# Decode block with sliding-window attention: value caches loaded and multiplied four heads at a time instead of two, and the output weights in wide products throughout

## Chip, cores, metric

One core of one Trainium2 chip runs one launch of the kernel. The metric is device time in microseconds (us), the median of several runs. All data is fp32.

## What is computed

Two sequences, one new token each, model width 512. A conditioning vector gives six rows of modulation; then attention over the last 4096 entries of the caches (32 query heads, 8 key/value heads of 128), then a SiLU feed-forward of width 1792.

```python
mod = (silu(c) @ w_mod).reshape(2, 6, 1, 512)          # sa, ca, ga, sb, cb, gb
h = layernorm(x) * (1 + ca) + sa
q = (h @ wq) in 32 heads of 128
k, v = the last 4096 entries of each cache, each of the 8 heads used by 4 query heads
o = softmax(q k^T / sqrt(128)) v
x = x + ga * (o @ wo)
h = layernorm(x) * (1 + cb) + sb
out = x + gb * (silu(h @ w1) @ w2)
```

The caches' windows are 2 x 8 x 4096 x 128 values each, 33.6 MB for keys and as much for values; `wq` and `wo` are 8.4 MB each, `w_mod` 6.3 MB, `w1` and `w2` 3.7 MB each. All of it is read once.

## The kernel before, in words

**The ring.** Nearly everything that is read goes through one tile `slots` of 8 slots of 16 KB per partition (L68). `stream(n)` (L70) hands out the next n slots, aligned to n where n is even. Every load is issued by SP, in program order, and waits there until the instructions that read the slots' former content have ended; a later load cannot pass an earlier one. `w_mod` takes slots 0 to 2, `wq` slots 4 to 7, and then the caches follow.

**The steps.** Attention is cut into 8 steps. A step is two key/value heads of one sequence: `load_pair` (L77) brings 4096 x 2 x 128 values as 32 KB per partition in two slots, partition p holding a run of 64 cache entries of one head. The loop (L477) is a hand-written order on each engine (`inorder` keeps it), with the values one step behind the keys:

- `keys(s, j)` (L356): VectorE turns a quarter of the keys in 32x32 blocks by two stream transposes into a tile kT (pool `ktp`, 4 buffers, L55).
- `scores(s, j)` (L366): four TensorE products of 32 output columns by 512, one for each 32-row stripe of the PSUM tile `s`.
- `maxima(s)` (L382) and `exponentials(s)` (L400): VectorE takes row maxima `mx`; TensorE turns them (`mT`); VectorE joins and spreads them (`mg`, `mrow`); TensorE spreads them over the partitions (`bp`); ScalarE copies that (`bias`) and takes exp into `pr`, with row sums.
- `turn(s)` (L415): VectorE transposes `pr` (`xp`) and spreads it (`zp`); TensorE places it (`pT`, 4 products by 256); ScalarE writes the two masked copies `ptb` (two buffers, one for odd and one for even steps).
- `weighted(s)` (L442): 16 products of 32 columns by 512 of `ptb` and the values, on four 32-column stripes in turn, summed in `o`; ScalarE copies the sum to `ob` at once.
- `collect(s)` (L460): four products of 64 columns by 128 pick each head's rows from `ob` and add them up in `o_all`.

In a round of the loop TensorE does the first quarter of scores of step s, then turn(s-1), collect(s-2), the other three quarters, the maxima and exponentials of s, and then the value products of step s-1 (L477 to L499). So value products run while VectorE and ScalarE are busy with the next step's softmax.

**place(n)** (L312) spreads the queries of key/value heads 4n to 4n+3 over `qbd`; place(1) comes in the round of s = 2.

**The rest.** After the loop, `o_all` is divided by the row sums into `on` (L536), turned to `oTn` (L539 to L543), and TensorE does 6 products whose result nobody reads (`busy(6)`, tile `junk`, L576). `wo` lies in slots 0 to 3: the first 28 of its 32 runs are multiplied 512 wide and added up in four stripes (`acc_o`, L577), the last four in 128-wide pieces straight into `ao` (L586); `gather` (L546) copies `acc_o` out, one half by ScalarE and one by VectorE, and adds the stripes into `ao`. Then follow the second layernorm, `w1` (slots 4 to 6, tile `hid`), SiLU, `w2` (slots 7, 0, 1, 2; tiles `acc_yw`, `acc_y`, `acc_l`), another gather, and the output's DMA (L704).

Of the kernel before, what the change touches and what calls it, by code (L numbers as in the profile page):

```python
# [13 lines left out]
P = 128  # L14
# [9 lines left out]
def adaln_block(  # L24
# [30 lines left out]
    ktp = ctx.enter_context(tc.tile_pool(name="ktp", bufs=4))  # L55
# [21 lines left out]
    def load_pair(cache, s):  # L77


        i, b = divmod(s, B)  # L80
        t = stream(2)
        nc.sync.dma_start(
            t,
            cache[b, 2 * i : 2 * i + 2, SK - W :, :].rearrange("e (u n) d -> u e (n d)", u=P // 2),
        )
        return t
# [16 lines left out]
    for b in range(B):  # L103
# [46 lines left out]
    id16, mix = const([P, 16], "id16"), const([P, 16, 2], "mix")  # L150
# [3 lines left out]
    nc.gpsimd.tensor_mul(  # L154
        mix,
        id16[:, :, None].to_broadcast([P, 16, 2]),
        half[:, None, :].to_broadcast([P, 16, 2]),
    )
    odd = const([P, 2], "odd")
    nc.vector.tensor_reduce(  # L160
        odd, ident.rearrange("p (a r) -> p r a", r=2), axis=AX.X, op=ALU.add
# [13 lines left out]
    selh = const([P, 4, 4 * HQ - 8], "selh")  # L175
    nc.gpsimd.memset(selh, 0.0)
    nc.gpsimd.tensor_copy(
        selh[:, :, 2 * HQ - 8 : 2 * HQ].rearrange("p m (e g) -> p m e g", e=2),
        id4.rearrange("p (e m g) -> p m e g", e=2, g=G),
# [26 lines left out]
    ptb = [const([P, 16, 2, 16], f"ptb{i}") for i in range(2)]  # L206
# [132 lines left out]
    o_all = bank("O", "o_all")[:, :DH]  # L339
# [9 lines left out]
    def fetch(s):  # L349

        if s < STEPS:
            kt[s] = load_pair(k_cache, s)
        if s > 0:
            vt[s - 1] = load_pair(v_cache, s - 1)
# [11 lines left out]
    def scores(s, j):  # L366
# [3 lines left out]
        i, b = divmod(s, B)  # L370
        for c in range(2):
            for e in range(2):
                r, h = 64 * e + 32 * c, 2 * i + e
                inorder(nc.tensor.matmul(  # L374
                    s_ps[s][r : r + 32, :],
                    qbd[h // 4][:, h % 4, b, j, :],
                    kT[s, j][:, 32 * c : 32 * c + 32, e:32:2],
                    start=(j == 0),
                    stop=(j == 3),
                ))  # L380
# [34 lines left out]
    def turn(s):  # L415
# [9 lines left out]
        tp = bank("C", f"pT{s}")[:, : 2 * P]  # L425
        for i in range(4):
            inorder(nc.tensor.matmul(  # L427
                tp[32 * i : 32 * i + 32, :],
                mix.rearrange("p v e -> p (v e)"),
                zp.rearrange("p y t x -> p (y t) x")[:, :, 4 * i : 4 * i + 4],  # L430
                start=True,
                stop=True,
            ))
        for e in range(2):
            inorder(nc.scalar.activation(  # L435
                ptb[s % 2][:, :, e, :],
                tp.rearrange("p (w z) -> p w z", z=16),
                AF.Copy,
                scale=odd[:, e : e + 1],
            ))  # L440

    def weighted(s):  # L442


        o_ps[s] = bank("D", f"o{s}")
        for w in range(16):
            r = 32 * (w % 4)
            inorder(nc.tensor.matmul(  # L448
                o_ps[s][r : r + 32, :],
                ptb[s % 2][:, w].rearrange("p e z -> p (e z)"),  # L450
                vt[s].rearrange("p (c w m f d) -> p c f w m d", c=2, w=4, m=4, f=2)[
                    :, w // 8, w // 4 % 2, w % 4
                ],
                start=(w < 4),
                stop=(w >= 12),
            ))
        o_sb[s] = once.tile([P, 4 * DH], F32, tag="wide", name=f"ob{s}")
        inorder(nc.scalar.copy(o_sb[s], o_ps[s]))  # L458

    def collect(s):  # L460

        i, b = divmod(s, B)
        lo = 2 * HQ - 8 - (HQ * b + 2 * G * i)
        for m in range(4):
            r = 64 * (m % 2)
            inorder(nc.tensor.matmul(  # L466
                o_all[r : r + 64, :],
                selh[:, m, lo : lo + 2 * HQ],
                o_sb[s][:, m * DH : (m + 1) * DH],
                start=(s == 0 and m < 2),  # L470
                stop=(s == STEPS - 1 and m >= 2),
                skip_group_check=True,
            ))

    fetch(0)
    keys(0, 0)
    for s in range(STEPS + 1):  # L477
        if s < STEPS:
            fetch(s + 1)
            scores(s, 0)  # L480
        if s > 0 and s != STEPS - 1:
            turn(s - 1)
        if s > 1:
            collect(s - 2)
        if s == 2:
            place(1)
        if s < STEPS:
            for j in range(1, 4):
                keys(s, j)
                scores(s, j)  # L490
            maxima(s)
            exponentials(s)
        if s < STEPS - 2:
            keys(s + 1, 0)
        if s > 0:
            weighted(s - 1)
        if s == STEPS - 2:
            turn(s)
            keys(s + 1, 0)  # L499
    collect(STEPS - 1)  # L500
# [12 lines left out]

    rx = once.tile([P, B, HKV // 2, 2, G], F32, tag="rx", name="rx")
    for b in range(B):
        nc.vector.tensor_mul(
            rx[:, b],
            rowsum[:, b:STEPS:B, None, None].to_broadcast([P, HKV // 2, 2, G]),
# [3 lines left out]
    for r in (0, 64):  # L522
        nc.tensor.matmul(
            lp[r : r + 64, 0:1],
            rx.rearrange("p b i e g -> p (b i e g)"),
            ones,
            start=True,
            stop=True,
        )
    rl = once.tile([P, 1], F32, tag="rl", name="rl")  # L530
# [201 lines left out]
```

## Time and profile before

| | |
|---|---|
| median of 3 runs | 235.44 us (235.41 to 235.5) |
| profiled execution, first to last instruction (its span; the page lists no other time for it) | 233.7 us |
| TensorE products (PE) | 161.1 us busy, 69% |
| VectorE (DVE) | 115.6 us busy, 49% |
| ScalarE (ACT) | 28.5 us busy, 12% |
| moved by DMA | 97.68 MB, 418 GB/s over the span |
| granted TensorE clock, mean | 0.934 |

PE's busy time counts products that run side by side on different columns once. A product of fp32 values shows as two instructions, so "x32" beside a row of value products means 16 products of the code. PEld are the loads of the stationary operand. A row of the timeline gives start, duration, engine, line, operation, output and inputs, the count merged into the row, and in brackets how long the engine had been idle before and what released it. "The span's start" is time zero of all of them.

### The profile page before, as it was taken

What the parts mean: (1) busy time and instruction counts of PE and PEld (TensorE: products, weight loads), DVE (VectorE), ACT (ScalarE), POOL (GpSimd) and SP (SyncE); (2) the same over time, 40 slices, a digit from 0 to 9 for tenths busy, and PEclk for the clock granted to TensorE, in tenths of its full rate; (3) what the DMA queues carried; (4) which work ended last, traced back from release to release, by engine and by line L of the source; (5) the groups of instructions that cost most, each with busy time, mean ns of one, the idle gap of its engine ahead of it and who ended that gap; (6) DMA issues with size and microseconds to landing.
All of it is one profiled execution on the core that took longest, in us unless ns stands there. A gap on an engine that the chain in (4) does not pass through costs nothing.

```text
span 233.7 us, 2571 instructions
## 1 busy us (share of the span) xinstructions
PE 161.1 (69%) x1070; PEld 43.3 (19%) x1070; DVE 115.6 (49%) x179; ACT 28.5 (12%) x64; POOL 10.5 (4%) x35
## 2 busy tenths in 40 slices
PE   0004916859577839797598749759759779789684
PEld 0001401201111111211120201202112122324222
DVE  0007240278894758695197089259559540101232
ACT  2000210000311120120210201111020120102020
POOL 2004710000000000000000000000000000000000
PEclk9999985979999977999979999988997997999999
DMA  7998998999999999999999999999999999989991
GB/s 269 446 542 359 404 494 359 446 444 421 415 421 449 446 437 415 426 426 446 449 437 409 418 437 449 449 421 412 426 444 449 443 421 437 463 367 437 424 404 57
DMA packets 3794, 97.68 MB, mean 418 GB/s; under 512 B 432, under 2 KB 456, under 8 KB 968
## 3 DMA queue, kind: packets, MB, share of 16 engines
q1 hardware_dynamic: 3768, 97.53, 97.1%
q8 instruction: 8, 0.13, 0.2%
q14 instruction: 2, 0.02, 0.0%
q10 hardware_dynamic: 16, 0.00, 0.0%
HBM read 97.53 MB, written 0.00 MB: 417 GB/s over the span
## 4 chain that ended last, share of the span: by engine, by line
DMA 60%; issue 18%; DVE 14%; PE 6%; POOL 0%; SPq 0%; POOLq 0%; ACT 0%
DMA slots<-in_A_k_cache_dram 22%; DMA slots<-in_A_wq_dram 15%; DMA slots<-in_A_v_cache_dram 12%; DMA slots<-in_B_w_dram 12%; DVE kT L361 11%; PE o L448 2%; PE q L302 2%; DVE zp L420 1%; PE acc_yw L661 1%; DVE xp L418 1%; PE qr L323 0%; PE acc_y L671 0%; DVE qT L315 0%; POOL qg L319 0%; SPq L109 0%
## 5 line engine op out<-in xcount | busy, mean ns | idle before, releaser
L361 DVE STREAM_TRANSPOSE kT<-slots 128x1024 f32<-128x1024 f32 x64 | 73.7, 1212 | 23.7 <-DMA slots<-in_A_k_cache_dram 23.6
L374 PE MATMUL s<-kT,qbd 128*32 128x512 f32 x256 | 68.6, 693 | 19.1 <-DVE kT L361 18.0
L448 PE MATMUL o<-slots,ptb 128*32 128x512 f32 x256 | 30.8, 624 | 2.1 <-DMA slots<-in_A_v_cache_dram 2.1
L374 PEld LDWEIGHTS s<-kT,qbd 128*32 128x32 f32 x256 | 9.6, 113 | 68.4 <-DVE kT L361 63.4
L269 PE MATMUL m_a<-slots,scT 128*32 128x256 f32 x32 | 4.4, 506 | 20.5 <-DVE scT L261 20.5
L302 PE MATMUL q<-slots,hq_T 128*32 128x512 f32 x64 | 8.3, 680 | 7.0 <-DMA slots<-in_A_wq_dram 7.0
L448 PEld LDWEIGHTS o<-slots,ptb 128*32 128x32 f32 x256 | 8.1, 114 | 17.9 <-issue 17.8
L404 ACT COPY bias<-bp 128x1 f32<-128x1 f32 x8 | 1.3, 159 | 77.0 <-PE bp L402 77.0
L384 DVE TENSOR_REDUCE mx<-s 128x1 f32<-128x512 f32 x8 | 5.5, 691 | 9.6 <-PE s L374 9.6
L565 PE MATMUL junk<-quad,id 128*32 128x512 f32 x22 | 10.2, 595 | 0.0
L420 DVE TENSOR_TENSOR zp<-xp,quarter 128x1024 f32<-128x1024 f32 x8 | 9.8, 1225 | 0.2
L435 ACT ACTIVATE ptb<-pT,odd 128x256 f32<-128x256 f32 x16 | 6.7, 472 | 25.6 <-PE pT L427 25.6
L255 DVE STREAM_TRANSPOSE cT<-xc 128x128 f32<-128x128 f32 x1 | 0.4, 401 | 16.7 <-DMA xc<-in_c_dram 16.7
L427 PE MATMUL pT<-zp,mix 128*32 128x256 f32 x64 | 5.7, 428 | 3.6 <-DVE zp L420 3.5
L458 ACT COPY ob<-o 128x512 f32<-128x512 f32 x8 | 4.7, 585 | 26.1 <-PE o L448 26.1
L272 PE MATMUL m_sp<-slots,scT 128*32 128x512 f32 x32 | 7.4, 738 | 0.0
L386 PE MATMUL mT<-ident,mx 128*1 128x128 f32 x16 | 3.0, 270 | 6.3 <-DVE mx L384 6.3
L315 DVE STREAM_TRANSPOSE qT<-q 128x512 f32<-128x512 f32 x2 | 1.4, 717 | 11.7 <-PE q L302 10.2
L418 DVE STREAM_TRANSPOSE xp<-pr 128x512 f32<-128x512 f32 x8 | 5.5, 686 | 3.4 <-ACT pr L406 3.4
L579 PE MATMUL acc_o<-slots,oTn 128*32 128x512 f32 x56 | 6.2, 593 | 0.7 <-DMA slots<-in_A_wo_dram 0.7
L466 PE MATMUL o_all<-ob,selh 128*64 128x128 f32 x64 | 6.0, 316 | 0.8 <-ACT ob L458 0.8
L550 DVE COPY acc_o_sb<-acc_o 128x256 f32<-128x256 f32 x1 | 0.4, 425 | 12.4 <-ACT acc_o_sb L549 12.4
(140 smaller groups left out, 93.8 us busy)
## 6 DMA issues: line engine op xcount, KB each, us to landing
slots<-in_A_k_cache_dram SPq DMA_DIRECT2D x8, 4096.0 KB, 27.4
slots<-in_A_v_cache_dram SPq DMA_DIRECT2D x8, 4096.0 KB, 27.6
slots<-in_w_mod_dram SPq DMA_DIRECT2D x1, 6144.0 KB, 17.1
slots<-in_A_wo_dram SPq DMA_DIRECT2D x1, 6144.0 KB
slots<-in_B_w_dram SPq DMA_DIRECT2D x1, 2688.0 KB
slots<-in_A_wo_dram SPq DMA_DIRECT2D x1, 2048.0 KB, 29.5
slots<-in_B_w_dram SPq DMA_DIRECT2D x1, 2048.0 KB
slots<-in_B_w_dram SPq DMA_DIRECT2D x1, 896.0 KB
```

Of the source, the lines that this page charges most:

```text
L272: nc.tensor.matmul(m_sp[r, :], scT[:, k, :], cd[:, g], start=(k == 0), stop=(k == 3))
L302: nc.tensor.matmul(q_ps[n][32 * g : 32 * g + 32, :], hq_T[:, k, :], wv[:, n, g], start=(k == 0), stop=(k == 3),)
L361: inorder(nc.vector.transpose(kT[s, j][:, 32 * c : 32 * c + 32, :], kt[s].rearrange("p (n j r) -> p j n r", j=4, r=32)[:, j, 32 * c : 32 * ...
L374: inorder(nc.tensor.matmul(s_ps[s][r : r + 32, :], qbd[h // 4][:, h % 4, b, j, :], kT[s, j][:, 32 * c : 32 * c + 32, e:32:2], start=(j == ...
L418: inorder(nc.vector.transpose(xp, pr[s]))
L420: inorder(nc.vector.tensor_mul(zp, xp[:, None, :, 0:16].to_broadcast([P, 4, 16, 16]), quarter[:, :, None, None].to_broadcast([P, 4, 16, 16 ...
L427: inorder(nc.tensor.matmul(tp[32 * i : 32 * i + 32, :], mix.rearrange("p v e -> p (v e)"), zp.rearrange("p y t x -> p (y t) x")[:, :, 4 * ...
L435: inorder(nc.scalar.activation(ptb[s % 2][:, :, e, :], tp.rearrange("p (w z) -> p w z", z=16), AF.Copy, scale=odd[:, e : e + 1],))
L448: inorder(nc.tensor.matmul(o_ps[s][r : r + 32, :], ptb[s % 2][:, w].rearrange("p e z -> p (e z)"), vt[s].rearrange("p (c w m f d) -> p c f ...
L466: inorder(nc.tensor.matmul(o_all[r : r + 64, :], selh[:, m, lo : lo + 2 * HQ], o_sb[s][:, m * DH : (m + 1) * DH], start=(s == 0 and m < 2) ...
L565: inorder(nc.tensor.matmul(junk[0:32, :], id4, quad.rearrange("p m y -> p (m y)"), start=True, stop=True,))
L579: inorder(nc.tensor.matmul(acc[32 * g : 32 * g + 32, :], oTn[:, q, :], wot[q], start=(q < 4), stop=(q >= 24),))
```

## The change

Keys still come two heads at a time, but a step is now two heads of the same sequence as its neighbour (steps 0 to 3 are the first sequence, 4 to 7 the second). Two steps make a group of four heads.

- **Loads.** Values come for four heads in one load of 64 KB per partition in four slots. The ring then holds keys in slots 0 to 3 and values in slots 4 to 7 all through the loop. `fetch_values(i+1)` stands after `weighted(i)`, in the same four slots.
- **Order.** `turn(s)` follows the exponentials of its own step. `weighted(i)` follows the turn of the group's second step, then `collect(i)`, and the next step's keys and scores come after it. `ktp` has 3 buffers instead of 4.
- **turn.** `pT` is 8 products by 256 instead of 4, and the two `ptb` writes of a step are 512 wide instead of 256; `ptb` is one buffer that holds a whole group.
- **weighted.** 32 products of 64 columns by 512, on two 64-column stripes in turn. ScalarE copies the sum to `ob` in four masked pieces of 128.
- **collect.** One product of 64 columns by 512. The four 128-wide pieces are added by one VectorE reduction (`of_all`) after the loop.
- **wo.** All 32 runs are multiplied 512 wide; both halves of each `gather` are copied by ScalarE, with one more unread product after the first one's copies.
- Constants are made to fit (`mix`, `quad4`, `selh`, `own`). place(1) comes in the round of s = 1.

```diff
-    ktp = ctx.enter_context(tc.tile_pool(name="ktp", bufs=4))
+    ktp = ctx.enter_context(tc.tile_pool(name="ktp", bufs=3))
...
+    def load_heads(cache, b, h, heads):
+        t = stream(heads)
         nc.sync.dma_start(
             t,
+            cache[b, h : h + heads, SK - W :, :].rearrange("e (u n) d -> u e (n d)", u=P // heads),
         )
...
+        tp = bank("C", f"pT{s}")
+        for f in range(2):
+            for i in range(4):
+                inorder(nc.tensor.matmul(
+                    tp[32 * i : 32 * i + 32, 2 * P * f : 2 * P * (f + 1)],
...
+    def weighted(i):
...
+        for w in range(32):
+            r = 64 * (w % 2)
             inorder(nc.tensor.matmul(
+                o_ps[i][r : r + 64, :],
+                ptb[:, w].rearrange("p e z -> p (e z)"),
+                runs[:, w // 8, w // 4 % 2, w % 4],
+                start=(w < 2),
+                stop=(w >= 30),
+            ))
...
         for m in range(4):
+            c = slice(m * DH, (m + 1) * DH)
+            inorder(nc.scalar.activation(
+                o_sb[i][:, c], o_ps[i][:, c], AF.Copy, scale=own[:, m : m + 1]
+            ))
...
+        inorder(nc.tensor.matmul(
+            o_all, selh[:, lo : lo + 2 * HQ], o_sb[i], start=(i == 0), stop=(2 * i + 2 == STEPS)
+        ))
...
+    for s in range(STEPS):
+        scores(s, 0)
+        for j in range(1, 4):
+            keys(s, j)
+            scores(s, j)
+        fetch_keys(s + 2)
+        maxima(s)
+        exponentials(s)
+        if s % 2 == 0:
+            keys(s + 1, 0)
+        turn(s)
+        if s == 1:
             place(1)
+        if s % 2:
+            weighted(s // 2)
+            fetch_values(s // 2 + 1)
+            collect(s // 2)
+            if s + 1 < STEPS:
+                keys(s + 1, 0)
...
+    nc.vector.tensor_reduce(
+        of_all, o_all.rearrange("r (m d) -> r d m", m=4), axis=AX.X, op=ALU.add
+    )
...
-    for q in range(28):
+    for q in range(32):
...
-    for q in range(28, 32):
...
-    gather(ao, acc, "acc_o_sb", False, True)
+    gather(ao, acc, "acc_o_sb", True, True, fill=1)
```

How the change moves instructions on TensorE, at the first value products: before (s1 and s2 are the scores of steps 1 and 2, o0 the value products of step 0; the digits behind the last underscore only tell tiles apart):

```order
L374 MATMUL s1_337<-kT1_3_367,qbd0_151 32x512 x4
L386 MATMUL mT1_376<-ident_90,mx1_374 1x128
L402 MATMUL bp1_381<-negscale_141,mrow1_146 128x1
L448 MATMUL o0_390<-slots_80,ptb0_149 32x512 x16
L374 MATMUL s2_411<-kT2_0_387,qbd0_151 32x512 x4
L427 MATMUL pT1_420<-zp1_418,mix_111 32x256 x4
L466 MATMUL o_all_286<-ob0_407,selh_120 64x128 x4
L323 MATMUL qr1_437<-qg1_154,rep4_98 128x128
L374 MATMUL s2_411<-kT2_1_443,qbd0_151 32x512 x4
```

And now, at the first value products (o0 is the first group, steps 0 and 1):

```order
L440 MATMUL pT1_397<-zp1_395,mix_111 32x256 x8
L330 MATMUL qr1_414<-qg1_156,rep4_98 128x128
L462 MATMUL o0_420<-slots_80,ptb_152 64x512 x32
L480 MATMUL o_all_288<-ob0_453,selh_121 64x512
L386 MATMUL s2_463<-kT2_0_460,qbd1_154 32x512 x4
L386 MATMUL s2_463<-kT2_1_468,qbd1_154 32x512 x4
L386 MATMUL s2_463<-kT2_2_475,qbd1_154 32x512 x4
L386 MATMUL s2_463<-kT2_3_482,qbd1_154 32x512 x4
L398 MATMUL mT2_492<-ident_90,mx2_490 1x128
```

The value products stood between a step's softmax inputs (bp1) and its pT, and belonged to the step before. Now they stand behind the pT of their own group's second step, and the next step's first scores stand behind them and behind the collecting product.

On SP, the last loads of the caches and the first of the weights, before:

```order
L82 DMA slots<-in_A_v_cache_dram 128x1x8192
L82 DMA slots<-in_A_k_cache_dram 128x1x8192
L82 DMA slots<-in_A_v_cache_dram 128x1x8192 x2
L93 DMA slots<-in_A_wo_dram 128x12288
L93 DMA slots<-in_A_wo_dram 128x4096
L93 DMA slots<-in_B_w_dram 128x5376
```

And now:

```order
L81 DMA slots<-in_A_v_cache_dram 128x1x16384
L81 DMA slots<-in_A_k_cache_dram 128x1x8192 x2
L81 DMA slots<-in_A_v_cache_dram 128x1x16384
L92 DMA slots<-in_A_wo_dram 128x12288
L92 DMA slots<-in_A_wo_dram 128x4096
L92 DMA slots<-in_B_w_dram 128x5376
```

Before, key and value loads of one size took turns all through the loop. Now two key loads and one value load of twice the size come four times, and each value load stands behind the value products of the group before.

196 lines of the change are left out of this document (75 added, 121 removed).

## The prediction

> **What bounds the kernel now.** First the page's second part, for the shape over time, its third for the queue that loads (packets, MB, share), and its fourth, the chain that ended last.
>
> ```profile
> DMA  7998998999999999999999999999999999989991
> q1 hardware_dynamic: 3768, 97.53, 97.1%
> DMA 60%; issue 18%; DVE 14%; PE 6%; POOL 0%; SPq 0%; POOLq 0%; ACT 0%
> ```
>
> The DMA engines are busy in every slice but the last, and 60% of the chain is waiting for transfers. The windows between landings give the rate (columns: stretch, its length, PE, PEld, DVE, ACT, POOL busy, granted clock, DMA share, GB/s):
>
> ```profile
> 77.10:115.70 38.60, 29.45 (x186) 6.99 (x178) 25.87 (x31) 5.82 (x15) 0.49 (x2) 0.91 1.01 434
> 115.70:154.50 38.80, 29.05 (x168) 6.47 (x168) 24.12 (x26) 4.72 (x12) 0.00 (x0) 0.96 1.00 432
> 154.50:193.20 38.70, 29.96 (x188) 7.56 (x188) 26.62 (x32) 5.37 (x14) 0.00 (x0) 0.91 1.01 433
> ```
>
> Four 4.19 MB loads take 38.7 us. No engine comes near that, and each step's compute ends early: in the timeline VectorE waits for keys.
>
> ```profile
> 77.15 2.37 DVE L361 STREAM_TRANSPOSE kT<-slots 128x1024 f32<-128x1024 f32 x2 [2.71 <-DMA slots<-in_A_k_cache_dram]
> 135.39 2.37 DVE L361 STREAM_TRANSPOSE kT<-slots 128x1024 f32<-128x1024 f32 x2 [5.79 <-DMA slots<-in_A_k_cache_dram]
> ```
>
> A step lasts 19.3 us by the transfers and some 13.6 by the compute. What decides is whether a group of two steps, in the new order, still fits into 38.7 us.
>
> **The new group, step by step.** The old order hid the value products behind the next step's softmax. In the new one TensorE does them after the group's last turn, and the next group's scores queue behind them; VectorE can only run three key tiles ahead. So the group is one chain. Its pieces, from the middle of the loop:
>
> ```profile
> 96.01 3.64 PE L448 MATMUL o<-slots,ptb 128*32 128x512 f32 x32
> 98.78 0.67 DVE L418 STREAM_TRANSPOSE xp<-pr 128x512 f32<-128x512 f32 x1
> 99.49 1.23 DVE L420 TENSOR_TENSOR zp<-xp,quarter 128x1024 f32<-128x1024 f32 x1
> 100.63 6.87 DVE L361 STREAM_TRANSPOSE kT<-slots 128x1024 f32<-128x1024 f32 x6
> 100.86 0.64 PE L427 MATMUL pT<-zp,mix 128*32 128x256 f32 x8 [0.31 <-DVE zp L420]
> 101.56 0.84 ACT L435 ACTIVATE ptb<-pT,odd 128x256 f32<-128x256 f32 x2 [1.20 <-PE pT L427]
> 108.69 0.69 DVE L384 TENSOR_REDUCE mx<-s 128x1 f32<-128x512 f32 x1 [1.19 <-PE s L374]
> 110.10 0.18 DVE L395 COPY mrow<-mg 1x64 f32<-1x64 f32 x1
> 110.95 0.69 ACT L406 ACTIVATE pr<-s,bias 128x512 f32<-128x512 f32 x1
> 111.53 0.19 ACT L406 ACTIVATION_READ_ACCUMULATOR pr<-s,bias 128x1 f32 x1
> L448 PE MATMUL o<-slots,ptb x32: 592/592/617, 74.9 to 77.9; 128*32 128x512 f32 x32
> ```
>
> The pace first: 32 instructions in 3.64 us are eight rounds of four side by side, the last one 0.59 long: (3.64 - 0.59)/7 = 0.436 us a round. From the first score product C of a group:
>
> - Three key tiles wait ready. The fourth needs the first one's buffer: one tile's scores 0.436 + 0.59, about 0.07 to start, two transposes 2.37, and 1.2 until `mx`: **4.7**.
> - `mx` to the end of `mrow` 110.28 - 108.69 = 1.59, then the next step's first two transposes 2.37, then `xp`: **4.0** (exp ends earlier, at 111.72 - 108.69 = 3.0).
> - `xp` of the even step to exp's end of the odd one: 111.72 - 98.78 = **12.9**.
> - `xp` to `pT`: 100.86 - 98.78 = **2.1**.
> - `pT` to `ptb` 0.70, and two more rounds of half width for twice the products, 0.44: **1.1**.
> - Two `ptb` writes: 512 wide as `pr`'s 0.69; two of 256 started 0.84 - 0.47 = 0.37 apart, so of 512 some 0.6: **1.3**.
>
> Together 26.1 us. Next the products, which no row shows in this form. What rows show is a 64-column product 128 wide:
>
> ```profile
> 199.43 0.42 PEld L466 LDWEIGHTS o_all<-ob,selh 128*64 128x64 f32 x8 [1.66 <-ACT ob L458]
> 199.44 0.66 PE L466 MATMUL o_all<-ob,selh 128*64 128x128 f32 x8 [0.75 <-ACT ob L458]
> ```
>
> At a quarter of the width a round is 0.109; eight in a row would take 0.87 and more, two by two 3 x 0.109 + 0.27 = 0.60. Measured is 0.66, so 64-column products run two abreast, where 32-column ones run four abreast. A group has 64 instructions: 32 rounds, 31 x 0.436 + 0.59 = **14.1 us**, where two old steps took 7.3. Bounds: 7.1 if four ran abreast, 27.9 if none; I take the row's pace. Then `ob` in four pieces, between 0.6 (one 512-wide copy, below) and 1.5 (four of 0.37), I take 1.1 and 0.1 to start; the collecting product holds its columns two rounds, 0.87, before the next scores: **2.1**.
>
> A group is 26.1 + 14.1 + 2.1 = **42.3 us, more than the transfers' 38.7**. The kernel would go from transfers to this chain.
>
> Do the transfers add more? A value load is issued when the products before it end, and has the 26.1 us until its own products; its 8.39 MB take 19.4. What a load takes before its bytes flow shows in the first one, when the queue was empty:
>
> ```profile
> slots<-in_w_mod_dram SPq DMA_DIRECT2D x1, 6144.0 KB, 17.1
> ```
>
> 6.29 MB at 434 GB/s are 14.5 us, so 2.6 to start. That leaves 26.1 - 22.0 = 4 us of slack. Key loads wait only for transposes and come earlier. I charge **nothing**; the cover is those 4 us, and what exceeds them would come on top of each group.
>
> **The first group** begins as before: loads come in the same bytes (keys 0, 1, then values, complete where key load 2 landed before, 77.15). VectorE's order until the second exp is the old one:
>
> ```profile
> 75.16 0.69 ACT L406 ACTIVATE pr<-s,bias 128x512 f32<-128x512 f32 x1
> 75.75 0.19 ACT L406 ACTIVATION_READ_ACCUMULATOR pr<-s,bias 128x1 f32 x1
> ```
>
> 75.94 + 2.1 + 1.1 + 1.3 + 14.1 = **94.5** for the end of the first value products; place(1) runs beside `pT` and `ptb`. Three more groups: 94.5 + 126.9 = **221.4** for the last ones, which ended at 198.69 before.
>
> **The tail.**
>
> ```profile
> 198.80 0.58 ACT L458 COPY ob<-o 128x512 f32<-128x512 f32 x1 [7.53 <-PE o L448]
> 200.14 0.61 DVE L536 TENSOR_SCALAR on<-o_all,rlb 128x128 f32<-128x128 f32 x2 [9.17 <-PE o_all L466]
> 201.91 5.34 PE L565 MATMUL junk<-quad,id 128*32 128x512 f32 x12
> 207.91 6.22 PE L579 MATMUL acc_o<-slots,oTn 128*32 128x512 f32 x56 [0.66 <-DMA slots<-in_A_wo_dram]
> 214.23 0.37 ACT L549 COPY acc_o_sb<-acc_o 128x256 f32<-128x256 f32 x1 [14.85 <-PE acc_o L579]
> 215.65 0.32 DVE L604 STREAM_TRANSPOSE aoT<-ao 128x128 f32<-128x128 f32 x1 [0.52 <-PE ao L552]
> 217.11 1.04 PE L565 MATMUL junk<-quad,id 128*32 128x512 f32 x2
> 219.46 1.71 PE L627 MATMUL hid<-slots,hT_b 128*32 128x448 f32 x16 [1.30 <-DMA slots<-in_B_w_dram]
> 225.36 0.21 DVE L657 TENSOR_TENSOR uT<-z,sgh 128x28 f32<-128x28 f32 x1
> 226.44 1.92 PE L661 MATMUL acc_yw<-slots,uT 128*32 128x512 f32 x16 [0.76 <-DMA slots<-in_B_w_dram]
> ```
>
> Before, `acc_o`, `hid` and `acc_yw` each waited for a load. Now `wo`, in the key slots, is issued before the last value products, so nothing waits for it; `w1` starts at once after them and needs some 11 us, `w2` 20, less than the compute ahead of each. So the tail is compute, from the last value product: `ob` and collect 0.1 + 1.1 + 1.03 = 2.2; `of_all`, nearest `mx`, 0.7 (bounds 0.3, one `on` instruction, and 1.4, twice `mx`); `on` until junk 201.91 - 200.14 = 1.8; 12 junk instructions, until now free because `wo` was late, 12 x 0.436 = 5.2; `acc_o` with 64 instead of 56 instructions 6.22 + 0.87 = 7.1; to `aoT` 215.65 - 214.13 = 1.5 (two ScalarE copies run about as one on each engine); to `hid`, behind two junk instructions, 217.11 + 0.87 - 215.65 = 2.3; `hid` to the end of `uT` 225.57 - 219.46 = 6.1; from `acc_yw` to the end 233.7 - 226.44 = 7.3. With the roundings 34.3, against 35.0 before with its waits. The `ao` products saved (1.1) are in it, and gains are thus small.
>
> 221.4 + 34.3 = 255.7 with TensorE at full clock.
>
> **The clock.** It does not stay there.
>
> ```profile
> 153.25 0.58 ACT L458 COPY ob<-o 128x512 f32<-128x512 f32 x1 [2.63 <-PE o L448]
> 155.87:158.94 3.07, 3.05 (x9) 0.38 (x9) 3.04 (x4) 0.00 (x0) 0.00 (x0) 0.51 1.06 459
> 193.35 5.34 PE L448 MATMUL o<-slots,ptb 128*32 128x512 f32 x32 [2.11 <-DMA slots<-in_A_v_cache_dram]
> 120.18 1.08 PE L427 MATMUL pT<-zp,mix 128*32 128x256 f32 x8
> 136.70:139.00 2.30, 2.17 (x8) 0.28 (x8) 2.27 (x3) 0.00 (x0) 0.00 (x0) 1.00 1.05 456
> 136.69 2.22 PE L374 MATMUL s<-kT,qbd 128*32 128x512 f32 x8 [3.09 <-DVE kT L361]
> ```
>
> After 2.6 us without a product (153.2 to 155.87) the granted clock was 0.51 for 3 us; value products after 2.1 us cost 5.34 instead of 3.64, and a `pT` at low clock 1.08 instead of 0.64. In the new group TensorE has, between the odd step's last scores and `pT`, 0.1 + 3.0 + 2.1 = 5.2 us with only `mT` and `bp`. Bounds a group: nothing, or pT's 2 x 0.44 and 1.70, that is 2.6. As the 3 us are partly used up by `pT` (2.1) and the wait for `ptb` (1.3), I take 0.9 + 0.3 = **1.2, four times: 4.8**.
>
> The Trainium skill, "TensorE: Matmul & The Clock Gate", section "What's actually happening", says that the clock halves after at least one idle window of about 3.4 us; `mT` and `bp` break the new gap, whose longest empty piece would be 3.2 us, so by it the sum stays at 255.7. The trace went to 0.51 after 2.6 us, and I follow the trace.
>
> Sum: 255.7 + 4.8 = 260.5 of span; the timed median lies 235.44 - 233.7 = 1.7 above its span: **262 us**.
>
> **Rivals.**
>
> 1. *The clock holds* through the gaps: 255.7 + 1.7 = 257.4. For it: the scores at 136.69, after 3.09 us without a product, ran at 1.00. Against it: after the two shorter gaps above products ran at half clock. By the Trainium skill's rule above this is the outcome.
> 2. *Full price of the clock*, 4 x 2.6: 268.
> 3. *Four 64-column products abreast*, or whatever makes a group's products 7 us: a group needs 36.5, the transfers bound it, the keys of step 6 land nine loads of 4.19 MB after 77.1, at 77.1 + 9 x 9.67 = 164.1, and from there eight transposes 2.37 + 6.87, 1.2 to `mx`, the five terms from 4.0 to 1.3 above (21.4), 7.1 and the clock's 1.2 give 204; with tail and 1.7, 240. Against it: the `o_all` rows.
> 4. *No two abreast*: 4 x 13.8 more, 317. The same rows speak against it.
> 5. *Faster*: the kernel stays with its transfers, and twelve cache loads have fewer boundaries than sixteen. That decides only from the point where a group's chain fits into the transfers' 38.7 us and the last value products end by 198.7, as before. Then 97.53 MB at 434 GB/s take 224.7, where the last load was waited for until 226.3 (226.44 less a start-up of 0.1): 235.4 - 1.6 = 233.8. Against it: DMA shares of 1.00 show no gap at a boundary. The Trainium skill, "DMA: Bandwidth & Descriptors", section "Anatomy of one DMA", has about 2 us fixed for every transfer; four fewer would be 8 us, which would give 227; the shares disagree, as queued loads overlap it.
>
> **How the numbers follow.** Forecast 0.62; clock holds 0.20; full price 0.09; products in 7 us 0.05; serial 0.02; faster 0.02. The range takes in 257.4 less `ob` and `of_all` at their lower bounds (4 x 0.5 + 0.35) and something for `ptb`, and 268 with the upper ones: **252 to 270**. A run of this kernel tells 0.2% from no change; only the last rival is faster, and within 0.2% lies only what falls between the third rival and it: faster 0.02, same 0.02, slower 0.96.
>
> **What would show it.** Right: the chain of waits turns from DMA to PE and DVE; value products of about 14 us a group, 42 to 44 us from one group's to the next; the clock near 0.5 at `pT`; DMA slices below 9 in the loop; `acc_o` right behind junk, waiting for nothing. Wrong: VectorE or the products waiting for DMA in the loop (then my slack of 4 us is gone), products of 7 or 28 us, or `acc_o` waiting for `wo`.

## The result, and the profile after

The changed kernel takes **271.67 us** (median of 5 runs, 271.26 to 272.15) against 235.44 us (235.41 to 236.25) of the kernel before on the same chip. The ratio is 1.1529, with a 95% interval of 1.1512 to 1.1547: 36.2 us slower. The forecast was 262 us and its range ended at 270, so the direction and the serial chain came as forecast, and the size came out 9.7 us too small. Times here and below are medians of undisturbed executions: of the four of run e1 the profiled one ran at a lower clock (317.17 us) and is left out.

The profiled execution has a span of 270.0 us (before 233.7) and a mean granted clock of 0.858 (before 0.934). These are the lines of its page that answer to those shown of before: the clock and the DMA share in 40 slices, the load queue, the chain that ended last, and the value products' group of instructions.

```profile
PEclk9999957797775999795799959599986869979998
DMA  9899899999999947999975998993899899994200
q1 hardware_dynamic: 3192, 97.53, 85.4%
PE 64%; DVE 13%; DMA 13%; ACT 6%; issue 2%; SPq 0%; DVEq 0%; ACTq 0%
L462 PE MATMUL o<-slots,ptb 128*64 128x512 f32 x256 | 62.9, 654 | 4.1 <-ACT ptb L448 4.1
```

Three things are to be seen. The DMA row, almost all eights and nines before, now dips once in each of the first three groups (to 4, 5 and 3 tenths) and ends early. The same 97.53 MB occupy their engines for 85.4% of a longer span instead of 97.1%. And the chain is PE for 64% instead of 6%: it goes through products and softmax, and transfers hold 13% of it, where they held 60%.

One whole group, the second, reads in the timeline like this:

```profile
99.24 1.14 ACT L472 ACTIVATE ob<-o,own 128x128 f32<-128x128 f32 x4 [15.25 <-PE o L462]
100.43 1.07 PE L480 MATMUL o_all<-ob,selh 128*64 128x512 f32 x2 [1.30 <-ACT ob L472]
101.43 4.69 PE L386 MATMUL s<-kT,qbd 128*32 128x512 f32 x32
106.17 0.69 DVE L396 TENSOR_REDUCE mx<-s 128x1 f32<-128x512 f32 x1 [1.19 <-PE s L386]
109.98 0.66 DVE L430 STREAM_TRANSPOSE xp<-pr 128x512 f32<-128x512 f32 x1
...
123.01 0.71 DVE L430 STREAM_TRANSPOSE xp<-pr 128x512 f32<-128x512 f32 x1 [1.54 <-ACT pr L418]
125.12 1.93 PE L440 MATMUL pT<-zp,mix 128*32 128x256 f32 x16 [3.16 <-DVE zp L432]
127.11 1.26 ACT L448 ACTIVATE ptb<-pT,quad 128x512 f32<-128x512 f32 x2 [4.14 <-PE pT L440]
128.43 15.75 PE L462 MATMUL o<-slots,ptb 128*64 128x512 f32 x64 [1.38 <-ACT ptb L448]
```

Each step begins where the one ahead of it ends, and the products wait for `ptb`, never for a transfer (the dots stand for the even step's turn and the odd step's scores). From the first row of the group to its products nothing on the chain is a load. The four groups' products are these (the first began right behind `qr`):

```profile
82.70 16.43 PE L462 MATMUL o<-slots,ptb 128*64 128x512 f32 x64
173.43 15.44 PE L462 MATMUL o<-slots,ptb 128*64 128x512 f32 x64 [1.38 <-ACT ptb L448]
218.12 15.28 PE L462 MATMUL o<-slots,ptb 128*64 128x512 f32 x64 [1.38 <-ACT ptb L448]
```

With the one above, they end at 99.13, 144.18, 188.87 and 233.40: a group takes 45.05, 44.7 and 44.5 us, where two steps took 38.7. From the last end to the end of the span stand 36.6 us (35.0 before).

### The profile page after: what moved, and what is told of

Read it like the earlier page. It is cut to its first block, busy times and chain, and to the rows that moved or that the text cites. A ratio compares the mean times of both kernels' runs of the same rounds, so it can differ in the third digit from the quotient of the medians.

```text
span 270.0 us, 2539 instructions
## 1 busy us (share of the span) xinstructions
PE 183.7 (68%) x1054; PEld 56.9 (21%) x1054; DVE 115.4 (43%) x180; ACT 32.6 (12%) x74; POOL 10.3 (4%) x35
## 3 DMA queue, kind: packets, MB, share of 16 engines
q1 hardware_dynamic: 3192, 97.53, 85.4%
HBM read 97.53 MB, written 0.00 MB: 361 GB/s over the span
## 4 chain that ended last, share of the span: by engine, by line
PE 64%; DVE 13%; DMA 13%; ACT 6%; issue 2%; SPq 0%; DVEq 0%; ACTq 0%
PE o L462 23%; PE s L386 17%; DMA slots<-in_A_wq_dram 13%; PE pT L440 6%; PE junk L557 4%; PE q L309 4%; DVE zp L432 4%; DVE kT L373 3%; PE acc_o L587 3%; DVE mx L396 2%; DVE xp L430 2%; ACT ptb L448 2%; ACT ob L472 2%; PE o_all L480 2%; ACT pr L418 1%
## 5 line engine op out<-in xcount | busy, mean ns | idle before, releaser
L462 PE MATMUL o<-slots,ptb 128*64 128x512 f32 x256 | 62.9, 654 | 4.1 <-ACT ptb L448 4.1
L386 PE MATMUL s<-kT,qbd 128*32 128x512 f32 x256 | 47.3, 736 | 2.5 <-DVE kT L373 2.3
L440 PE MATMUL pT<-zp,mix 128*32 128x256 f32 x128 | 15.5, 632 | 26.4 <-DVE zp L432 25.4
L462 PEld LDWEIGHTS o<-slots,ptb 128*64 128x64 f32 x256 | 19.4, 152 | 47.0 <-issue 40.2
L386 PEld LDWEIGHTS s<-kT,qbd 128*32 128x32 f32 x256 | 11.4, 129 | 35.9 <-issue 17.9
L448 ACT ACTIVATE ptb<-pT,quad 128x512 f32<-128x512 f32 x16 | 10.1, 683 | 35.2 <-PE pT L440 35.2
L557 PE MATMUL junk<-quad,id 128*32 128x512 f32 x24 | 12.7, 663 | 0.0
L472 ACT ACTIVATE ob<-o,own 128x128 f32<-128x128 f32 x16 | 4.6, 368 | 62.0 <-PE o L462 62.0
L440 PEld LDWEIGHTS pT<-zp,mix 128*32 128x32 f32 x128 | 5.5, 158 | 30.0 <-issue 30.0
L480 PE MATMUL o_all<-ob,selh 128*64 128x512 f32 x8 | 4.3, 618 | 5.0 <-ACT ob L472 5.0
```

What stands on the lines that cost most here:

```text
L386: inorder(nc.tensor.matmul(s_ps[s][r : r + 32, :], qbd[h // 4][:, h % 4, b, j, :], kT[s, j][:, 32 * c : 32 * c + 32, e:32:2], start=(j == ...
L440: inorder(nc.tensor.matmul(tp[32 * i : 32 * i + 32, 2 * P * f : 2 * P * (f + 1)], mix[:, f].rearrange("p u a e -> p (u a e)"), zp.rearrang ...
L448: inorder(nc.scalar.activation(ptb[:, :, e, :], tp.rearrange("p (w z) -> p w z", z=16), AF.Copy, scale=quad4[:, e : e + 1],))
L462: inorder(nc.tensor.matmul(o_ps[i][r : r + 64, :], ptb[:, w].rearrange("p e z -> p (e z)"), runs[:, w // 8, w // 4 % 2, w % 4], start=(w < 2),
L472: inorder(nc.scalar.activation(o_sb[i][:, c], o_ps[i][:, c], AF.Copy, scale=own[:, m : m + 1]))
L557: inorder(nc.tensor.matmul(junk[0:32, :], id4, quad.rearrange("p m y -> p (m y)"), start=True, stop=True,))
```

## The experiments

The theory, A: a group is one serial chain, its products of 14 us stand in it, and the clock that falls ahead of them lengthens them. The rivals were that the loads of four heads starve the transfers (C), and that the place of the products in the order alone, not their length, costs the time (D).

All were timed against the kernel before on their own chip, in 235.5 or 235.63 us.

| run | base | median, us | ratio to before, 95% interval |
|---|---|---|---|
| e4, the order alone | before | 241.62 | 1.025 (1.0235 to 1.0266) |
| e5, wide `wo` alone | before | 235.93 | 1.0016 (1.0007 to 1.0025) |
| e9, the ring alone | before | 235.61 | 1.0005 (0.9996 to 1.0014) |
| e11, second gather alone | before | 235.70 | 1.0006 (0.9997 to 1.0015) |
| e2, half the products' width | changed | 245.07 | 1.0396 (1.0363 to 1.0429) |
| e8, clock held, no `junk` | changed | 256.67 | 1.0912 (1.0877 to 1.0947) |
| e1, clock held | changed | 263.07 | 1.117 (1.1151 to 1.1189) |
| e3, no `junk` | changed | 267.19 | 1.1339 (1.132 to 1.1358) |
| e12, one late load more | changed | 271.62 | 1.1525 (1.1499 to 1.155) |
| e10, products moved behind | changed | 275.46 | 1.1701 (1.1665 to 1.1738) |

### e1 and e8: the clock held through the gaps

Unread products (`fill`) are put on TensorE in the gaps of each group's second step, on the bank of `o`, which the group's own first products clear again. e8 leaves out the six unread `junk` products ahead of `acc_o` as well.

```diff
+    def fill(s, *widths):
+        if s % 2:
...
+                inorder(nc.tensor.matmul(
+                    o_ps[s // 2][0:32, :n],
...
+        fill(s, 512)
...
+        fill(s, 256)
...
+        fill(s, 512, 512, 512, 256)
...
+        fill(2 * i + 1, 512)
...
-    busy(6)
```

> The changed kernel with products whose result nobody reads, put into the stretches of the odd steps in which TensorE has only mT and bp: one 512 wide before mT, one 256 wide behind it, 3.5 behind bp, one 512 wide between pT and the value products. They write the value products' own PSUM tile, which the first value products then overwrite. Theory A (the chain of the group, its clock under-priced): the granted clock stays near 1.0 from the odd step's scores to the value products, pT takes 1.1 us instead of 1.94 and the value products 14.0 instead of 15.3 to 16.4, four times; 4 x 0.85 + 6.5 less, 261.8 us. Theory B (64-column products and the longer pT are slow in themselves): the clock rises but pT and the products keep their times, 271.7. Theory C (loads that wait are what lengthens the groups): 271.7, with the products waiting for DMA.

e1 measured 263.07 us (1.3 more than A's figure), 8.6 less than the changed kernel. The trace shown is that of e8.

> Both cures at once: the unread products in the odd steps' gaps of the run with the clock kept up, and no unread products ahead of the wo products. Theory A: the two gains add up, 263.25 - 4.5 = 258.8 us, in the profile pT 1.1 us and the value products 14.0 us four times, at a granted clock near 1.0. If both were one effect of the clock: 262 or more.

e8 measured 256.67 us, 2.1 below A's figure. Its timeline, and its windows from 115 us on (length, busy time of PE, PEld, DVE, ACT and POOL, granted clock, DMA share, GB/s):

```profile
121.80 1.07 PE L456 MATMUL pT<-zp,mix 128*32 128x256 f32 x16
124.25 13.95 PE L478 MATMUL o<-slots,ptb 128*64 128x512 f32 x64 [0.56 <-ACT ptb L464]
166.59 13.95 PE L478 MATMUL o<-slots,ptb 128*64 128x512 f32 x64 [0.57 <-ACT ptb L464]
208.93 13.96 PE L478 MATMUL o<-slots,ptb 128*64 128x512 f32 x64 [0.36 <-ACT ptb L464]
```

```profile
115.00:124.00 9.00, 7.64 (x40) 2.26 (x38) 3.41 (x7) 2.01 (x5) 0.00 (x0) 1.00 1.04 448
124.00:138.00 14.00, 13.75 (x64) 4.51 (x64) 6.88 (x6) 0.20 (x1) 0.00 (x0) 1.00 0.89 383
```

The clock is at 1.00 through the gap and the products. The products then take 13.95 us, `pT` 1.07, and a group 208.93 - 166.59 = 42.3: the three figures that the forecast worked out for a held clock (14.1, 1.1 and 42.3), to 0.2 us. So what the loop of the changed kernel has above that is the clock's, and theory B, by which the 64-column products and the longer `pT` are slow in themselves, falls.

### e3: without `junk`

```diff
-    busy(6)
```

> The changed kernel without the six unread products ahead of the wo products. Theory A (wo has long landed, so they stand on the path): wo products start 6 us earlier, but the first 3 us of them at half clock (1.6 lost): 4.5 us less, 267.2. If the wo products wait for their load or the clock loss eats it all: 271.7.

It measured 267.19, as forecast. The 12 `junk` instructions, free while `wo` was late, now stand on the path; without them `acc_o` runs cold at first (granted clock 0.50 from 240.3 to 243.7) and gives a part back:

```profile
239.26 8.77 PE L586 MATMUL acc_o<-slots,oTn 128*32 128x512 f32 x64 [0.36 <-DVE oTn L548]
```

### e2: products of half the width

Each value product covers 256 of its 512 columns, so half of the values' part is left out; loads, instruction counts and order stay.

```diff
-                o_ps[i][r : r + 64, :],
+                o_ps[i][r : r + 64, 0:256],
...
-                runs[:, w // 8, w // 4 % 2, w % 4],
+                runs[:, w // 8, w // 4 % 2, w % 4, 0:2],
```

> The changed kernel with value products that move 256 of their 512 columns; half of the result's columns are left out, the copies read the computed half twice. Loads, waits and instruction counts stay. Theory A: the products fall from 15.7 to about 8 us, the group's chain from 44.7 to 37.5, less than the transfers' 38.7, so that the kernel is bound by its loads up to the last group; keys of step 6 land near 164, and from there 40 us to the end of the last products and 36 to the end: 240 to 243 us. Theory C: the loads set the time whatever the products take; over 265.

It measured 245.07 us, 26.6 less than the changed kernel and 2 above A's range. In its timeline the products take 8.5 to 9.6 us instead of 15.3 to 16.4, and VectorE waits for keys:

```profile
120.55 8.73 PE L462 MATMUL o<-slots,ptb 128*64 128x256 f32 x64 [1.38 <-ACT ptb L448]
125.93 9.15 DVE L373 STREAM_TRANSPOSE kT<-slots 128x1024 f32<-128x1024 f32 x8 [8.84 <-DMA slots<-in_A_k_cache_dram]
158.53 8.52 PE L462 MATMUL o<-slots,ptb 128*64 128x256 f32 x64 [1.38 <-ACT ptb L448]
197.26 9.62 PE L462 MATMUL o<-slots,ptb 128*64 128x256 f32 x64 [1.38 <-ACT ptb L448]
```

A group now takes 38.0 to 38.7 us, the transfers' pace. So with the same loads, the length of the products decides: theory C, by which the loads would hold the kernel back, falls here. The last products end at 206.9 (A's figure was 204), 8 us later than before, since the last group's chain stands behind the last keys.

### e4: the order alone

The kernel before, with the change's order: each step's turn, value products and collecting products follow its own exponentials. Loads and forms of the products stay.

```diff
-    for s in range(STEPS + 1):
...
+    for s in range(STEPS):
+        fetch(s + 1)
+        scores(s, 0)
...
+        maxima(s)
+        exponentials(s)
+        turn(s)
...
+        weighted(s)
+        collect(s)
```

> The kernel before with the changed kernel's order alone: turn, value products and collect of a step right behind its own softmax; loads, 32-column products four abreast and the rest as before. Theory A (the width of the value products decides, the order alone fits under the transfers): a step's chain is some 16 us against 19.3 of transfers, only the last step shows, 1 to 3 us: 236 to 238. Theory D (the order is what costs, whatever the products' width): the loss of overlap shows in each of the eight steps, 245 or more.

It measured 241.62 us, between the two theories' figures. The loop still goes at the transfers' pace, and its products wait for values:

```profile
125.84 6.37 PE L448 MATMUL o<-slots,ptb 128*32 128x512 f32 x32 [2.15 <-DMA slots<-in_A_v_cache_dram]
183.87 6.38 PE L448 MATMUL o<-slots,ptb 128*32 128x512 f32 x32 [1.88 <-DMA slots<-in_A_v_cache_dram]
202.57 5.56 PE L448 MATMUL o<-slots,ptb 128*32 128x512 f32 x32 [0.96 <-ACT ptb L435]
```

What it loses it loses at the end: the products ahead of the last wait for their values until 183.87, and only then the whole last step begins, whose products end at 208.1 instead of 198.7. Of these 9.4 us the tail gives 3.3 back: from there to the end it takes 31.7 us instead of 35.0, since nothing in it waits for a load any more. The compute that the old order had hidden is in the open once, not eight times.

### e9, e6: the ring alone

The kernel before with the change's order of heads and slots: keys in slots 0 to 3, values of two steps in slots 4 to 7. In a first form (e6, 239.82 us, ratio 1.0182, 1.0167 to 1.0198) the ring counted on: it handed two of the values' slots to the keys of step 4 and the keys' slots to the next values, while a part of the keys there was not turned yet. So some of the turned keys of step 3 were values, those of step 4 were the keys of step 5, and its time says little of the ring as meant; e9 lays it as meant, with two value loads of two heads each.

```diff
+    def load_two_pairs(cache, s):
...
+        t = slots[:, 4:8, :].rearrange("p s e -> p (s e)")
...
-    fetch(0)
+    fetch_keys(0)
+    fetch_keys(1)
+    fetch_values(0)
...
+            fetch_keys(s + 2)
...
+            if s % 2 == 0:
+                fetch_values(s)
```

> The kernel before with the change's ring alone: steps in the new order of heads, keys in slots 0 to 3, values of two steps in slots 4 to 7, whose two loads stand together behind the second step's value products; products, turn and collect as before, values a step behind the keys. Theory A: the queue stays full, since key loads are issued early and the products are short; 235.5 to 238. Theory C (the shared value slots starve the transfers): 245 or more, with DMA slices below 9 in the loop.

> The kernel before with the change's order of heads and its ring alone: keys in slots 0 to 3, values of two steps in slots 4 to 7, each value load behind the value products of the step whose slots it takes; the products, the turn and everything else as before. Theory A (the loss is the serial chain of a group, the ring costs little): the transfers stay without gaps until the last step, 235.5 to 238 us. Theory C (four slots that are filled, used and emptied in turn starve the transfers, whatever the products do): 245 us or more, with gaps in the DMA share in every group.

e9 measured 235.61 us, the same as before within the measurement. Its load queue's line and the chain that ended last, beside 97.1% and 60% before:

```profile
q1 hardware_dynamic: 3768, 97.53, 97.2%
DMA 61%; PE 26%; DVE 9%; issue 1%; ACTq 1%; ACT 1%; DVEq 0%
```

The transfers run through: four value slots that are filled and emptied in turn cost nothing while the products are short. Theory C falls a second time.

### e10, e7: the products behind the next exponentials

The changed kernel with a group's value products behind the first exponentials of the next group, where VectorE's transposes lie beside them. e7 (287.42 us, ratio 1.2204, 1.2182 to 1.2225) had e6's fault in the ring, by which here a part of the value products read keys as well; e10 lays the ring as meant.

```diff
+        if s > 0 and s % 2 == 0:
+            weighted(s // 2 - 1)
+            fetch_values(s // 2)
...
+            collect(s // 2 - 1)
...
-        if s % 2:
-            weighted(s // 2)
-            fetch_values(s // 2 + 1)
-            collect(s // 2)
```

> The changed kernel with the value products of a group moved behind the first exponentials of the next group, ahead of that step's turn, so that VectorE turns keys beside them; the value load of the group after follows them. Theory A: the products no longer stand in the chain with the softmax, but the value slots are filled, used and emptied one after the other: 19.4 + 2.6 + 14 us and the waits between make 36 to 38 us a group; value loads begin late, 258 to 262 us. Theory D (the order is what costs): near 240.

> The changed kernel with the value products of a group moved behind the first exponentials of the next group, and the ring laid as the change has it. Theory A (the serial chain costs the time, and what the order takes out of the chain comes back): the products of 14 us now lie beside VectorE's key transposes, but the next value load waits until they have ended, so the value slots are filled, used and emptied in turn and the DMA queue has gaps: 258 to 262 us. Theory D (only the place of the products in the chain matters, the transfers take what is left): near 240 us.

It measured 275.46 us: slower than the changed kernel, which neither theory said. Its page's DMA slices, and from the timeline the products, a wait for keys, and the last value load's issue on SP:

```profile
DMA  9899899999799807747999999989089989999600
```

```profile
106.40 13.95 PE L463 MATMUL o<-slots,ptb 128*64 128x512 f32 x64
143.12 13.95 PE L463 MATMUL o<-slots,ptb 128*64 128x512 f32 x64
153.59 2.37 DVE L374 STREAM_TRANSPOSE kT<-slots 128x1024 f32<-128x1024 f32 x2 [10.90 <-DMA slots<-in_A_k_cache_dram]
182.66 15.65 PE L463 MATMUL o<-slots,ptb 128*64 128x512 f32 x64 [1.08 <-ACT pr L419]
198.34 0.53 SPq L82 DMA_DIRECT2D slots<-in_A_v_cache_dram  x1
221.93 15.36 PE L463 MATMUL o<-slots,ptb 128*64 128x512 f32 x64 [9.53 <-DMA slots<-in_A_v_cache_dram]
```

Two things happened, and they pull apart. A group does get shorter: 36.7, 39.5 and 39.3 us from products to products instead of 45. That is close to the 36 to 38 that theory A had for e7, and D's 240 falls. But the first products begin at 106.4 instead of 82.7. Until they end the value slots stay full, and the key slots hold keys that VectorE has not turned yet (SP issues the next key load at 103.28): the slice from 95.5 to 102.3 us has a DMA share of 0. What was not loaded there is late afterwards, as far as the trace shows: VectorE waits 10.9 us for keys at 153.59, the last value load is issued at 198.34 (188.9 in the changed kernel), and the last products wait 9.5 us for it. The pace was won and the start lost; I had only looked at the pace.

### e5 and e11: the parts of the tail

e5 is the kernel before with all of `wo` 512 wide and both halves of the gathers on ScalarE; e11 only has the second gather's halves on ScalarE.

```diff
-    for q in range(28):
+    for q in range(32):
...
-    gather(ao, acc, "acc_o_sb", False, True)
+    gather(ao, acc, "acc_o_sb", True, True, fill=1)
```

```diff
-        inorder(nc.vector.tensor_copy(sb_[:, D // 2 :], wide[:, D // 2 :]))
+        second = nc.scalar.copy if name == "acc_y_sb" else nc.vector.tensor_copy
+        inorder(second(sb_[:, D // 2 :], wide[:, D // 2 :]))
```

> The kernel before with the change's last part alone: all 32 runs of wo 512 wide, both halves of each gather copied by ScalarE, one unread product behind the first one's copies. Theory A (the end is set by the last load, then by 7.3 us of compute): the wo products end 0.9 us later, which the wait for w1 (1.3 us) hides; the second gather is 0.2 us quicker, as in the changed kernel (4.41 against 4.63 us from acc_yw to the output's DMA): 235.2 to 235.5. If the wide products came onto the path: 236 or more.

> The kernel before with both halves of the second gather alone copied by ScalarE, nothing else changed. If that gather was quicker by this alone in the run with the wide output weights: 235.2 to 235.3 us, 0.2 less than the kernel before. If it was chance: 235.4 to 235.5 us.

e5 measured 235.93 us against 235.5, 0.16% slower, and I had expected 235.2 to 235.5. There the wide products wait for their load and then run cold (granted clock 0.50 from 208.9 to 212.3):

```profile
208.31 8.77 PE L581 MATMUL acc_o<-slots,oTn 128*32 128x512 f32 x64 [2.29 <-DMA slots<-in_A_wo_dram]
```

e11 measured 235.70 against 235.5, the same within the measurement and just above both forecasts. From the start of `acc_yw` to the issue of the output's DMA it takes 231.00 - 226.37 = 4.63 us, like the kernel before, where e5 takes 231.24 - 226.82 = 4.42 and the changed kernel 4.41. So the copies on ScalarE alone do not bring the 0.2 us. That e5 and the changed kernel agree speaks against chance; what does bring it is not shown.

### e12: a load ahead of the output's DMA

From the issue of the output's DMA to the end of the span the kernel before needs 2.6 us (231.07 to 233.7) and the changed one 3.9:

```profile
266.12 0.63 SPq L703 DMA_DIRECT2D out_dram<-yo  x1
```

The load queue has been empty before it for 13 us there (a DMA share of 0.01 from 253 to 266 us). e12 adds one load of 2.1 MB that nobody reads.

```diff
+    stream(1)
+    nc.sync.dma_start(stream(1), wq.rearrange("(p q) e -> p q e", q=4)[:, 0, :])
```

> The changed kernel with one more load of 2.1 MB, which nobody reads, into a slot of w1 behind the products of hid, so that the load queue has worked until shortly before the output's DMA. If the output's DMA takes 3.9 us to the end of the span instead of 2.6 because the queue was idle before it: 2.6 to 2.9 us again, and 270.5 to 270.9 us in all. If the load queue has nothing to do with it: 3.9 us again, 271.5 to 271.9 us.

It measured 271.62 us, no gain, and its output's DMA took 268.6 - 265.08 = 3.5 us though the queue had worked until shortly before (a DMA share of 0.80 from 258 to 265 us). And in e10, whose last two DMA slices are 0, it took 272.8 - 270.00 = 2.8. So the idle queue is not the cause. By their traces the runs built on the kernel before (e4, e5, e9, e11) take 2.5 to 2.6 us there, those built on the changed kernel 2.8 to 3.9; what makes the difference stays open.

## Why the prediction was right in kind and too small in size

**What bounds the kernel.** Right. The loop went from the transfers to one chain a group; the chain of waits turned from DMA to PE, and no product waited for a load. One of the signs of being wrong did appear: VectorE waited for keys in the loop, three times, 17.7 us in all. This is the longest wait:

```profile
132.72 6.88 DVE L373 STREAM_TRANSPOSE kT<-slots 128x1024 f32<-128x1024 f32 x6 [7.75 <-DMA slots<-in_A_k_cache_dram]
```

It cost nothing, because it lay beside the value products: the three key tiles were ready at 139.60, and the products ended at 144.18. So the sign was too wide, and the slack of 4 us was there. On the fifth rival: the section "Anatomy of one DMA" of the Trainium skill that it names gives its 2 us for DMAs issued by GpSimd, and the loads here are issued by SP.

**The steps of a group.** Right, to 0.2 us each: four key tiles to `mx` 106.17 - 101.43 = 4.74 (forecast 4.7), `mx` to `xp` 3.81 (4.0), `xp` to `xp` 123.01 - 109.98 = 13.03 (12.9), `xp` to `pT` 2.11 (2.1), `ptb` to the products 1.32 (1.3). `ob` and the collecting product came to 101.43 - 99.13 = 2.3 (2.1), and 2.25 twice after that, 0.5 over three groups.

**The products.** Right: two abreast, 13.95 us with the clock held (14.1). The rivals that had four or one abreast are out, and the width is the largest part: half of it in e2 takes 26.6 us away.

**The clock: the step that failed.** The prediction took "0.9 + 0.3 = 1.2, four times: 4.8": 0.9 for `pT` and 0.3 for the products, on the ground that the 3 us at low clock were nearly used up before the products began. The 0.9 was right, since `pT` took 1.94 instead of 1.1. The 0.3 was not: the products lost 1.2 to 2.3 us. These windows show the second group's gap and products, with what lies ahead and behind, and then the low stretches of the first, third and fourth group (columns as above):

```profile
115.02:121.85 6.83, 5.36 (x32) 1.15 (x24) 4.75 (x7) 0.28 (x1) 0.00 (x0) 1.00 0.91 391
121.85:132.09 10.24, 5.71 (x28) 1.89 (x29) 1.97 (x3) 2.20 (x5) 0.00 (x0) 0.50 1.02 442
132.09:155.98 23.89, 18.55 (x96) 5.32 (x92) 13.52 (x15) 2.08 (x7) 0.00 (x0) 1.00 0.78 320
77.48:87.72 10.24, 7.65 (x30) 2.68 (x32) 3.30 (x7) 1.78 (x4) 0.50 (x2) 0.50 1.04 446
169.64:176.46 6.82, 4.97 (x24) 1.70 (x26) 0.33 (x1) 1.26 (x2) 0.00 (x0) 0.50 1.01 434
214.01:220.84 6.83, 4.65 (x24) 1.54 (x26) 0.95 (x3) 1.26 (x2) 0.00 (x0) 0.50 1.06 461
```

In the second group the clock falls at 121.85 and stays at 0.50 until 132.09. `pT` runs all of its 1.9 us at it, the wait for `ptb` follows, and the clock rises only 3.7 us after the first value product; in the first, third and fourth group it is 5.0, 3.0 and 2.7 us. Half of that time is lost, 2.5, 1.8, 1.5 and 1.4 us in the order of the groups, and so the products took 16.43, 15.75, 15.44 and 15.28 us where e8's took 13.95. The prediction had its 3 us from a stretch of the kernel before in which TensorE worked without a pause (155.87 to 158.94, PE busy for 3.05 of 3.07 us). In the new gap PE is busy for 5.7 of 10.24 us. So the time at low clock is not a stock that runs out from its start: in these traces it ends only some microseconds into work without a pause, and `pT` alone was too short for that. The price is `pT`'s 1.94 against 1.1 four times and the products' excess over 14.1 (2.3, 1.65, 1.35 and 1.2): 3.4 + 6.5 = **9.9 us** instead of 4.8, or 2.5 a group. It is nearly the full bound of 2.6 that the second rival had, whose 268 was closer than the forecast's 262. e8, which puts products into the gap, brings the period back to the 42.3 forecast for a held clock.

The low stretches of this trace last 3.41 (even steps), 6.83 or 10.24 us, one, two or three times 3.41, and any two changes of the clock lie a whole number of such steps apart. The four groups do the same work, so what each pays seems to depend on where its gap falls on this raster; that is read from the traces, and no run was made to test it.

The Trainium skill, "TensorE: Matmul & The Clock Gate", section "What's actually happening", asks for at least one idle window of about 3.4 us for the clock to halve, and by that rule the first rival's 257.4 would have come. The measurement decides otherwise. From the last scores to the fall at 121.85 no empty stretch was longer than 0.8 us:

```profile
120.62 0.38 PE L398 MATMUL mT<-ident,mx 128*1 128x128 f32 x2 [0.79 <-DVE mx L396]
121.62 0.35 PE L414 MATMUL bp<-negscale,mrow 1*128 1x1 f32 x2 [0.61 <-DVE mrow L407]
```

**The tail.** Right that it is compute and that gains there are small; 36.6 us measured, 34.3 forecast. 1.0 of the difference is `junk` at low clock (238.23 to 244.52 for what should have taken 5.2; the granted clock is 0.50 until 241.3), 1.25 the output's DMA, which I had taken from before.

```profile
238.23 6.42 PE L557 MATMUL junk<-quad,id 128*32 128x512 f32 x11
244.52 7.43 PE L587 MATMUL acc_o<-slots,oTn 128*32 128x512 f32 x61
```

`acc_o` came right behind `junk` and waited for nothing, as forecast, and e3 confirms that these products are no longer free.

**Small terms missed.** I wrote that place(1) runs beside `pT` and `ptb`; its product `qr` waited for `ptb` and stood ahead of the first value products.

```profile
82.00 0.77 PE L330 MATMUL qr<-qg,rep 128*128 128x128 f32 x2 [1.42 <-ACT ptb L448]
```

That is 0.7 us, and the first `mx` came 0.55 later than before (59.10 against 58.55), behind slower products of `q` (10.00 us against 8.34).

The account: 5.1 of the clock beyond 4.8, 0.7 and 0.55 at the start, 0.5 of `ob` and collect, 1.0 and 1.25 in the tail make 9.1 us; 0.4 is not placed. The two make the 9.5 between the forecast's unrounded 262.2 (255.7 + 4.8 + 1.7) and the 271.67 measured.

**Where the 36.2 us are.** The runs make a ladder, though its rungs change more than one thing each: the order alone 6.1 (e4), grouped products of half the width 245.07, the full width with the clock held 11.6 more (e8), and the low clock with `junk` 15.0 on top. In the traces the last rung is 10.5 us until the last products (233.40 against 222.89) and 4.9 behind them. e1 and e8 differ by 6.4 us, while leaving out `junk` is worth 4.5 in e3. Behind the last products e3 and e8 both take 31.7 us instead of 36.6, so 4.9 of it is the tail in both; the rest must lie ahead of the last products, and without a trace of e1 at 263 us it stays open. No run was faster than the kernel before.

## What to carry to other kernels

Count a loop by its chain as soon as an order takes away the work that covered another: here a group's products stood open, though each engine was busy for less than 70% of the span. Where TensorE pauses for a few microseconds ahead of long products, price the low clock from the first pause until some three to five microseconds into unbroken products, with the short products in between at half speed as well, instead of subtracting them. And when products are moved later, look at the first round too: a buffer that is freed later can let the transfers stand still once, and they do not catch up.

## What the runs showed of the hardware that was not expected

- Two products of 0.35 and 0.38 us in a gap of some 5 us did not keep the clock up: it fell to 0.50 about 2 us after the last scores, with no empty stretch over 0.8 us until then.
- The clock came back only 2.7 to 5.0 us after the first of a group's value products (128.43 to 132.09 in the second group); 1.9 us of `pT` with a pause of 1.4 us behind it did not raise it. Stretches at 0.50 lasted 3.41, 6.83 or 10.24 us in the changed kernel's loop.
- The output's DMA, 4 KB, took 2.6 us from issue to the end of the span in the kernel before and 3.9 in the changed one, and neither a busy nor an idle load queue ahead of it explains that.
